# Products of token halves in three groups of the last block: seven for eight, in an attention and SwiGLU kernel

## Chip, cores and metric

One core of one Trainium2 chip runs the whole kernel. The metric is the device time of one execution in microseconds; three runs of the kernel before were timed, and the median counts.

## What is computed

```python
def reference(q, k, v, g_q, g_k, w_gate, w_val, w_out):      # q, k, v: (8, 12, 448, 64)
    scores = rmsnorm(q, g_q) @ rmsnorm(k, g_k).T / 8          # per batch and head
    x = softmax(scores) @ v                                   # heads side by side: (3584, 768)
    g = x @ w_gate                                            # (768, 1536)
    return (g / (1 + exp(-g)) * (x @ w_val)) @ w_out          # (1536, 768)
```

All of it is in float32.

## The kernel before

The function `fast` holds the kernel. The tokens are worked on in NB = 4 blocks of two batches (2 x 448 tokens). Each block has a *gate and value* stretch, x times both input matrices, and a *down* stretch, times the output matrix; the attention of the next two batches lies between the down products, and its preparation (squares, roots, transposes; `attention`, L736) reaches back into the gate and value stretch. The last block has no attention behind it.

The matrix products are made with a bilinear scheme that takes 15 products for 18 blocks: the two batches' tokens and three parts of the contraction are combined into 15 left sides, kept in the tile `xs` (L625), and the weights into 15 right sides, which the first block makes once and keeps in DRAM (`up_sides` L637, `down_sides` L638). The 15 are called by number; UP_ORDER (L627) is their order. The intermediate width of 1536 is cut into NG = 4 groups. So a gate and value stretch has 4 groups x 15 steps x 2 (gate and value) = 120 products (`up_product`, L1453). A product is NC2 = 2 calls of a 128x128 weight against 448 columns (L1474) and is planned at PRODUCT = 1.504 us (L665).

Each product accumulates onto a chain of earlier ones in its PSUM bank, and is read out after each step: by ScalarE as a copy (L1409) or by VectorE as a sum or difference with an earlier result (L1411, L1413, L1415), as UP_READ (L1394) says. Gate products use the two banks `mm`, value products the two banks `at`; chains are numbered so that steps alternate between the banks. Six results per group come out. For each, ScalarE takes the SiLU of the gate (L1551) and VectorE multiplies it with the value (L1554) into `gt`. The down products (`down_product`, L1639, matmul L1663) read `gt` and sums of it in `hs` (`combine`, L1612).

Weights for five steps are loaded from DRAM by one call of `up_load` (L1569) into one of two places `ws` (`load_sides`, L1417, DMAs at L1428), on the queue of SP. The rooms `work` (queries and keys, L580), `es` (softmax weights, L644) and `spare` are cut into named rings by `take` (L586).

The order of all work is made by a planner (`Order`, L365): each operation is added with an engine, a planned duration, a due time, what it comes after and which places it takes or uses; `run` goes through the engines and writes each engine's instructions out in the order in which they would start. On the chip every engine runs its own list in that order, and waits only for data and places. Due times come from block_start (L671), block_end (L674) and pair_time (L677).

Of the kernel before, what the change touches and what calls it, by code (L numbers as in the profile page):

```python
# [493 lines left out]
def fast(  # L494
# [45 lines left out]
    P = 128  # L540
# [27 lines left out]
        rr=4, ws=2, **{x + str(i): 1 for x in "vw" for i in range(6)},  # L568
# [14 lines left out]
    OFTEN = dict(w1=0, w2=1, w3=2, w4=3, rows=4)  # L583
# [82 lines left out]
    UP, DOWN, BOTH = 30 * NG * PRODUCT, 90.7, 170.0  # L666
# [3 lines left out]

    def block_start(n):  # L671
        return FIRST + n * (UP + BOTH) + MORE * (n > 0)

    def block_end(n):  # L674
        return block_start(n) + UP + MORE * (n == 0)
# [722 lines left out]
    }  # L1398
    DOWN_READ = {
# [17 lines left out]
    def load_sides(key, sides, part, sums):  # L1417

        n = 2 * (NC2 if sums is UP_SUMS else NG)
        to = take(*key, [P, WS])[:, 0 : n * len(part) * P]  # L1420
# [18 lines left out]
    def block(n):  # L1439
        add = order.add  # L1440
        start = block_start(n)
        unit = (block_end(n) - start) / (30 * NG)
# [10 lines left out]
        def up_product(g, step, x, which, load, key):  # L1453
            nonlocal last
            when = start + (2 * (15 * g + step) + which) * unit

            b = ("BCDAE".index(CHAIN[x]) % 2 if CHAIN[x] != "E" else 0) ^ (g % 2) ^ (n > 0)
            fresh = x in FRESH
            opens = which and g == 0 and step < 2
            at = place_of(x, UP_ORDER[step - step % 5 :][:5], UP_SUMS)  # L1460
            bank = (which, b)

# [5 lines left out]
            def emit():  # L1468
                if opens:
                    take(*value_banks[b], [P, TB])  # L1470
                w = tiles[key][:, 0 : 2 * NC2 * 5 * P]
                w = w.rearrange("p (w c x f) -> p w c x f", w=2, c=NC2, f=P)
                for c in range(NC2):
                    nc.tensor.matmul(  # L1474
                        ps(), w[:, which, c, at], xs[:, SLOT[x], c],
                        start=fresh and c == 0, stop=c == NC2 - 1, skip_group_check=True,
                    )
# [8 lines left out]
                uses=[key] + ([value_banks[b]] if which and not opens else []), mode="full",  # L1486
# [66 lines left out]
            def weigh():  # L1553
# [6 lines left out]
                "ACT", 0.55, when - 0.5, gate, after=[acc["gate", result]], takes=[act],  # L1560
# [5 lines left out]
                rank=60.0 * (n == 0),  # L1566
            )

        def up_load(g, piece):  # L1569
            key = ("ws", (n, g, piece))  # L1570
            load = add(
                "SP", 1.2, start + (30 * g + 10 * piece) * unit - 24.0,
                lambda: load_sides(key, up_sides[g], UP_ORDER[5 * piece :][:5], UP_SUMS),
# [289 lines left out]
```

## Time and profile before

| | |
|---|---|
| three runs | 1453.04, 1456.36, 1457.0 us; median 1456.36 us |
| span of the profiled execution | 1452.0 us, 19362 instructions (the page gives no other time for it) |
| TensorE matmul records | 6736, busy 1426.0 us |
| busy in the span: VectorE, ScalarE, GpSimd | 879.8, 601.6, 405.7 us |
| moved by DMA | 193.29 MB |

All times of the trace are counted from the start of the span. A `nc.tensor.matmul` call in float32 shows as two weight loads (PEld) and two matmul records (PE). DVE is VectorE, ACT ScalarE, POOL GpSimd; SPq is the DMA queue that SP issues to. Blocks start their gate and value stretches at about 124, 474, 827 and 1174 us.

### The profile page before, as it was taken

The page shows a single profiled execution, that of the slowest core. Times are in us where ns is not written, and L with a number is a line of the kernel's source. Part 1 is how long each engine was busy: PE and PEld are TensorE (multiplying, and loading weights), DVE is VectorE, ACT ScalarE, POOL GpSimd, SP SyncE. Part 2 cuts the span into 40 slices and gives each one's busy share as a digit, 9 for nine tenths or more (in the row PEclk, how much of TensorE's full clock was granted, in tenths as well). Part 3 has the DMA queues.
Part 4 walks back from the last instruction along what each step waited for, and adds up shares of the span by engine and source line. Part 5 has one row for each costly group of instructions (what it writes and reads, how often), then busy time and mean ns, then how long its engine had stood idle before and what let it go on. Part 6 is the DMA issues. An engine that isn't in the chain of part 4 may idle for free.

```text
span 1452.0 us, 19362 instructions
## 1 busy us (share of the span) xinstructions
PE 1426.0 (98%) x6736; PEld 689.5 (47%) x6736; DVE 879.8 (61%) x1485; ACT 601.6 (41%) x1210; POOL 405.7 (28%) x476
## 2 busy tenths in 40 slices
PE   8999999999999999999999999999999999999997
PEld 4455454534444455544444455544444445555553
DVE  5889876878866434546877642455686644442533
ACT  6875444476653222356564122345555322212100
POOL 4756666625443000022443200011434300000000
PEclk9999999999999999999999999999999999999999
DMA  7778979854643533433644623443463452322235
GB/s 196 217 219 268 352 266 310 260 149 90 129 103 64 133 102 92 114 113 70 122 98 86 138 74 107 107 112 93 85 126 77 95 135 73 108 73 90 69 100 110
DMA packets 410416, 193.29 MB, mean 133 GB/s; under 512 B 280004, under 2 KB 390852, under 8 KB 410308
## 3 DMA queue, kind: packets, MB, share of 16 engines
q1 hardware_dynamic: 399040, 190.57, 49.1%
q10 hardware_dynamic: 11140, 1.38, 0.7%
q8 instruction: 55, 0.90, 0.3%
q14 instruction: 53, 0.43, 0.1%
q0 software_dynamic: 128, 0.00, 0.0%
HBM read 157.29 MB, written 34.60 MB: 132 GB/s over the span
## 4 chain that ended last, share of the span: by engine, by line
PE 90%; DMA 3%; DVE 2%; ACT 2%; SPq 1%; issue 1%; POOL 1%; ACTq 0%; DVEq 0%; POOLq 0%
PE at L1474 25%; PE mm L1474 25%; PE mm L1663 23%; PE at L1049 8%; PE st L970 7%; PE st L1080 1%; PE mm L1080 1%; DMA out_dram<-spare 1%; SPq L768 1%; DMA work<-in_k_dram 1%; ACT es L985 1%; DMA xs<-in_moe_w_gate_dram 0%; PE st L908 0%; DMA v<-in_v_dram 0%; ACT work L918 0%
## 5 line engine op out<-in xcount | busy, mean ns | idle before, releaser
L1474 PE MATMUL at<-xs,ws 128*128 128x448 f32 x960 | 401.2, 540 | 2.5 <-DVE v L1413 1.4
L1474 PE MATMUL mm<-xs,ws 128*128 128x448 f32 x960 | 401.7, 541 | 0.2 <-DVE hs L1315 0.2
L1474 PEld LDWEIGHTS at<-xs,ws 128*128 128x128 f32 x960 | 181.4, 190 | 184.7 <-issue 166.7
L1474 PEld LDWEIGHTS mm<-xs,ws 128*128 128x128 f32 x960 | 182.2, 190 | 180.7 <-issue 177.9
L888 POOL TENSOR_TENSOR work<-work,rr 128x448 f32<-128x448 f32 x72 | 71.8, 1016 | 467.5 <-DVE rr L715 341.6
L1663 PE MATMUL mm<-gt,ws 128*128 128x448 f32 x448 | 175.5, 543 | 0.0
L970 PE MATMUL st<-work 64*64 64x448 f32 (+1 forms) x1536 | 151.2, 501 | 10.3 <-ACT work L918 4.9
L985 ACT ACTIVATE es<-st 128x896 f32<-128x896 f32 x129 | 114.2, 914 | 101.6 <-PE at L1049 87.8
L1411 DVE TENSOR_TENSOR gt<-gt,mm 128x448 f32<-128x448 f32 x64 | 39.7, 621 | 188.1 <-PE mm L1474 161.7
L1663 PE MATMUL mm<-hs,ws 128*128 128x448 f32 x384 | 151.3, 544 | 0.0
L990 POOL TENSOR_TENSOR sums<-es 128x896 f32<-128x896 f32 x36 | 77.2, 2145 | 176.8 <-PE st L1080 83.7
L1663 PEld LDWEIGHTS mm<-gt,ws 128*128 128x128 f32 x448 | 83.6, 190 | 83.0 <-issue 80.8
L1551 ACT ACTIVATE st<-gt 128x448 f32<-128x448 f32 x96 | 52.3, 547 | 159.1 <-DVE gt L1415 85.7
L1409 ACT COPY gt<-mm 128x448 f32<-128x448 f32 x80 | 42.6, 532 | 157.5 <-PE mm L1474 157.4
L1049 PE MATMUL at<-es,v 64*64 64x448 f32 (+1 forms) x1032 | 106.0, 507 | 0.0
L1663 PEld LDWEIGHTS mm<-hs,ws 128*128 128x128 f32 x384 | 71.3, 190 | 71.0 <-issue 70.1
L970 PEld LDWEIGHTS st<-work 64*64 64x64 f32 x1536 | 50.9, 133 | 79.1 <-issue 37.4
L1409 ACT COPY v<-at 128x448 f32<-128x448 f32 x96 | 51.0, 532 | 80.4 <-PE at L1474 79.6
L990 POOL TENSOR_TENSOR sums<-sums,es 128x896 f32<-128x896 f32 x36 | 76.0, 2112 | 2.8
L1049 PEld LDWEIGHTS at<-es,v 64*64 64x64 f32 (+1 forms) x1032 | 44.1, 134 | 56.2 <-issue 50.4
L1554 DVE SCALAR_TENSOR_TENSOR gt<-st,v 128x448 f32<-128x448 f32 x96 | 59.7, 622 | 7.3 <-DVE v L1415 0.5
L1411 DVE TENSOR_TENSOR v<-v,at 128x448 f32<-128x448 f32 x64 | 39.8, 621 | 39.6 <-PE at L1474 39.5
(170 smaller groups left out, 1550.5 us busy)
## 6 DMA issues: line engine op xcount, KB each, us to landing
ws<-up_sides SPq DMA_DIRECT2D x32, 1024.0 KB, 5.6
ws<-down_sides SPq DMA_DIRECT2D x16, 1024.0 KB, 5.7
ws<-down_sides SPq DMA_DIRECT2D x28, 512.0 KB, 4.8
ws<-up_sides SPq DMA_DIRECT2D x16, 768.0 KB, 4.9
out_dram<-spare SPq DMA_DIRECT2D x168, 56.0 KB, 2.1
v<-in_v_dram SPq DMA_DIRECT2D x96, 96.0 KB, 2.5
ws<-up_sides SPq DMA_DIRECT2D x32, 256.0 KB, 5.9
ws<-up_sides SPq DMA_DIRECT2D x16, 512.0 KB, 5.8
```

The source lines that it names most:

```text
L888: nc.gpsimd.tensor_tensor(out=tiles["t", m][:, x], in0=tiles["qk", (m, x)], in1=rr.to_broadcast([P, NC, C]), op=ALU.mult,)
L970: nc.tensor.matmul(st[ds(D * x, D), h, 0:n], tiles["KT", m][rows, ds(P * j + D * of_keys, D)], tiles["QT", m][rows, ds(Q * of_queries, n)] ...
L985: nc.scalar.activation(e, tiles["st", (m, j)][:, :, 0 : S * width(j) // P], AF.Exp)
L990: nc.gpsimd.tensor_tensor(out=to, in0=tiles["e", (m, 0)] if j == 1 else to, in1=e, op=ALU.add)
L1049: nc.tensor.matmul(tiles["at", (m, x)][ds(D * h, D), ds(0, Q) if early else queries], tiles["v", m][rows, j, h], tiles["e", (m, j)][rows, ...
L1080: nc.tensor.matmul(to[ds(D * h + C * x, C)], halves[:, x] if half else many[:, 0:C], term[:, h, 0:Q] if half else term[:, h, ts(x, Q)], st ...
L1409: nc.scalar.copy(to, ps)
L1411: nc.vector.tensor_tensor(out=to, in0=old, in1=ps, op=ALU.add)
L1474: nc.tensor.matmul(ps(), w[:, which, c, at], xs[:, SLOT[x], c], start=fresh and c == 0, stop=c == NC2 - 1, skip_group_check=True,)
L1551: nc.scalar.activation(take(*act, [P, 2, TB])[:, 0, 0:S], to, AF.Silu)
L1554: nc.vector.scalar_tensor_tensor(to, tiles[act][:, 0, 0:S], 1.0 / SCALE, tiles[ready], op0=ALU.mult, op1=ALU.mult,)
L1663: nc.tensor.matmul(banks[s][:, 0:S], w[:, s, g, at], where[x][:, g], start=fresh and g == 0, stop=g == NG - 1, skip_group_check=True,)
```

## The change

In the last block the order of the four groups' products changes, and groups 1 to 3 are computed in another way.

Group 0 is split: first its 15 gate products, at the end of the stretch its 15 value products. Between them come groups 1 to 3. For these, the tokens are cut into halves of 224 columns, and the two halves, the two parts of the contraction and the pair of gate and value make a 2 x 2 x 2 product, which is done in seven half products instead of eight. They run in four streams of each step: X (two half products: A11 and S2), Y (two: S1 and S3), Z (two: A12 and A22) and W (one: S4). Z and W follow two steps behind X and Y (LAG). Each stream has two PSUM banks.

GpSimd makes the sums S1 to S4 of token halves (`halves_of`), 60 operations of 224 columns, beside the gate products of group 0. S3 takes the place of half of `xs`, so `restore` puts that half back, 15 operations, before the value products. GpSimd also joins the streams' results for each of the six results of a group (`plus`, three to four operations of 224 columns and one of 448, the last of these on VectorE for three results of group 3), VectorE adds W's half (`top`), and the gate and the multiplication follow in place. Results of a group and the next have separate places for three to four of the six sums.

The seven right sides for each step are prepared in blocks 1 and 2 (`prepare`): 15 pieces of three steps, eight in block 1 and seven in block 2, 16 us apart. Each is loaded into `es` or the room of `t` and `QT` in turn, gets four subtractions of 384 columns on GpSimd and is stored in new DRAM tiles `up7`. In the last block they are loaded in pieces of three steps: four sides for X and Y (768 KB, three places) and three sides for Z and W (576 KB, two places), with `ws` and the room of `qk` as places.

The order of the table UP_SUMS changes so that three neighbouring steps lie together, and the place `ws` is one 128-column side wider. The sums of `gt` for the down products of all groups are made after the seven-product groups, since S1 lies in `hs`, and the down products take the groups in the order 1, 2, 3, 0. The core of the diff:

```diff
-        rr=4, ws=2, **{x + str(i): 1 for x in "vw" for i in range(6)},
+        rr=4, ws=2, **{x + str(i): 1 for x in "vw" for i in range(6)}, w6=1, **{x: 1 for x in ("xy0", "xy1", "xy2", "zw0", "zw1", "wl")},
...
-    OFTEN = dict(w1=0, w2=1, w3=2, w4=3, rows=4)
+    OFTEN = dict(w1=0, w2=1, w3=2, w4=3, rows=4, w6=7)
...
-    UP_SUMS = (8, 1, 7, 13, 10, 14, 3, 5, 11, 0, 4)
+    UP_SUMS = (8, 7, 1, 13, 10, 14, 3, 11, 4, 0, 5)
...
-    WS = 10 * NC2 * P
+    WS = 21 * P
...
+    SEVEN = {3: (1, 2, 3)}
+    HALF, LAG = S // 2, 2
+    up7 = {
+        g: dram.tile([P, 5, 7, 3, P], F32, name=f"up7_{g}")
+        for g in sorted({g for gs in SEVEN.values() for g in gs})
+    }
...
-    UP, DOWN, BOTH = 30 * NG * PRODUCT, 90.7, 170.0
+    DOWN, BOTH = 90.7, 170.0
...
+    SHORT = 40.0
+
+    def up_time(n, g=NG):
+        return sum(SHORT if i in SEVEN.get(n, ()) else 30 * PRODUCT for i in range(g))
...
+    PREPARE, PREPARE_PACE, up7_done = {1: [(g, u) for g in (1, 2, 3) for u in range(5)][:8], 2: [(g, u) for g in (1, 2, 3) for u in range(5)][8:]}, 16.0, {}
...
+        flat_hs = hs.rearrange("p s g t -> p (s g t)")
+        flat_es = es.rearrange("p n h t -> p (n h t)")
+        places_of = dict(S1=flat_hs, S2=work[:, 2 * NJ * 2 * D * 2 :], S4=flat_es)
+        held = [
...
+        def part_of(name, x):
+            tokens = slice(HALF, S) if name in ("A21", "A22", "S3") else slice(0, HALF)
+            if name[0] == "A" or name == "S3":
+                return xs[:, SLOT[x], int(name in ("A12", "A22")), tokens]
+            return places_of[name][:, ts(UP_ORDER.index(x), HALF)]
+
+        def halves_of():
+            for step, x in enumerate(UP_ORDER):
+                before = [old_done[x], *side_done[n, x], down_done.get(n - 1), clusters[EARLY * (n + 1) - 1, "total"]]
+                for i, (to, one, two, op) in enumerate((
+                    ("S3", "A11", "A21", ALU.subtract), ("S2", "A22", "S3", ALU.subtract),
+                    ("S1", "S2", "A11", ALU.add), ("S4", "A12", "S2", ALU.subtract),
+                )):
+                    done = order.add(
+                        "POOL", 0.66, start + (step + 1) * unit + 0.6 * i,
+                        lambda to=to, one=one, two=two, op=op, x=x: nc.gpsimd.tensor_tensor(
+                            out=part_of(to, x), in0=part_of(one, x), in1=part_of(two, x), op=op
+                        ),
+                        after=before, port=True, takes=held if step + i == 0 else [],
+                        uses=held if step + i else [],
+                    )
+                    before = [done]
+                    half_done[x, to] = done
+
+        def restore(now):
+            for step, x in enumerate(UP_ORDER):
+                side_done.setdefault((n, x), []).append(
+                    order.add(
+                        "POOL", 0.66, now - 3.0 + step * unit,
+                        lambda x=x: nc.gpsimd.tensor_tensor(
+                            out=part_of("A21", x), in0=part_of("A11", x), in1=part_of("S3", x),
+                            op=ALU.subtract,
+                        ),
+                        after=[third_done[x]], port=True, rank=30.0,
...
+        PARTS = dict(
+            X=((0, "A11"), (3, "S2")), Y=((2, "S1"), (1, "S3")),
+            Z=((0, "A12"), (2, "A22")), W=((1, "S4"),),
+        )
+        RESULT = {"t0": 0, "t1": 1, "d": 2, "t3": 3, "t4": 4, "t5": 5}
+
+        def sevens(begin_seven):
+            nonlocal last
+            q = PRODUCT / 4
+            steps, now = [], begin_seven
+            for k in range(15 * len(seven) + LAG):
+                for stream in "XYZW":
+                    j = k - LAG * (stream in "ZW")
+                    if 0 <= j < 15 * len(seven):
+                        steps.append((now, stream, j // 15, j % 15))
+                        now += q * len(PARTS[stream])
+
+
...
+            for (k, late), times in sorted(pieces.items(), key=lambda of: of[1][0]):
+                if late:
+                    at = (k - count) % 2
+                    name = f"zw{at}"
+                    base, tile_of = 12 * P, [ws_keys[at]]
+                else:
+                    at = (k - count + 2) % 3
+                    name = f"xy{at}"
+                    base, tile_of = (0, [ws_keys[at]]) if at < 2 else (4 * P, qk_keys)
+                key = name, (n, "seven", k)
...
+                    tiles[key] = room[:, base : base + (9 if late else 12) * P]
+                    src = up7[seven[k // 5]][:, k % 5, 4:7] if late else up7[seven[k // 5]][:, k % 5, 0:4]
...
+                g, x = seven[j], UP_ORDER[i]
+                b = ("BCDAE".index(CHAIN[x]) % 2 if CHAIN[x] != "E" else 0) ^ opening[stream == "Y"] ^ (j % 2)
+                bank = ({"X": 0, "Y": 1}.get(stream, stream), b)
+                fresh = x in FRESH
...
+                def emit(x=x, stream=stream, key=key, at=at, fresh=fresh, ps=ps, opens=opens, bank_tile=bank_tile):
+                    if opens:
+                        take(*bank_tile, [P, TB] if stream == "Y" else [P, 2, TB])
+                    w = tiles[key].rearrange("p (w x f) -> p w x f", x=3, f=P)
+                    for side, (slot, of) in enumerate(PARTS[stream]):
+                        nc.tensor.matmul(
+                            half(ps(), side), w[:, slot, at], part_of(of, x),
+                            start=fresh and side == 0, stop=True, skip_group_check=True,
...
+                    "PE", q * n_sides, when, emit,
+                    after=[
+                        load, last, free.get(bank),
+                        *(half_done[x, of] for _, of in PARTS[stream] if of[0] == "S"),
+                    ],
+                    takes=[bank_tile] if opens else [],
+                    uses=[key, *tile_of, *held] + ([bank_tile] if bank_tile and not opens else []), mode="full",
...
+                    if t == "t5" and other:
+                        return "sums", (n, g, t)
+                    if t == "t0" and other:
+                        return "v", (n, g, stream, t)
+                    if t == "t4" and other and (stream == "Y" or ends):
+                        return held[-1] if stream == "Y" else qk_keys[-1]
+                    if t == "t1" and other and stream == "Y":
+                        return "eh", (n, g, stream, t)
+                    X = {"t0": "v0", "t5": "v1", "t1": "v2", "t4": "v3", "t3": "v4", "d": "v5"}
+                    Y = {"t0": "w1", "t5": "w2", "t1": "w3", "t4": "w4", "t3": "rows", "d": "rows"}
...
+                    return order.add(engine, us, when, emit, after=after, uses=uses, port=True)
+
+                Xl, Xr, Yl, Yr, Wl = ("X", 0), ("X", 1), ("Y", 0), ("Y", 1), ("W", None)
+                closing = "DVE" if j == len(seven) - 1 and result in (2, 4, 5) else "POOL"
+                if stream == "X":
+                    ready7["X"] = plus(Xr, Xr, Xl, when + 1.0, [done], [kx])
+                elif stream == "Y":
+                    u4 = plus(Yl, Xr, Yl, when + 1.0, [done, ready7["X"]], [kx, ky])
+                    u3 = plus(Xr, Xr, Yr, when + 1.7, [u4], [kx, ky])
+                    ready7[g, result] = u3, plus(Yr, Yl, Yr, when + 2.4, [u3], [ky])
...
+                    def top(tile_at=tile_at, t=t):
+                        to = half(tile_at("Y", t), 0)
+                        of = flat_es[:, 15 * HALF :] if t == "t5" else tile_at("W", t)
+                        nc.vector.tensor_tensor(out=to, in0=to, in1=of, op=ALU.add)
+
+                    done = order.add(
+                        "DVE", 0.35, when + 3.0, top, after=[done, ready7[g, result][1]], uses=[ky, *(extra or [kw])], port=True, early=0.0, rank=20.0,
...
+                def load(four=four, part=part, g=g):
...
+                            for b in range(2):
+                                nc.sync.dma_start(
+                                    four[:, b, 0:2, ds(i * P, size * P)],
+                                    src[:, :, b].rearrange("p a x f -> p a (x f)"),
+                                )
+                            i += size
+
+                done = order.add(
+                    "SP", 1.0, when, load,
...
+                    moves=[transfer(2 * P, 4 * P * i) for i in groups(part, UP_SUMS) for _ in range(2)], early=0.0, **mine,
+                )
+                for i, (to, one, two) in enumerate(((2, 1, 0), (3, 5, 2), (1, 5, 1), (6, 4, 3))):
+                    done = order.add(
+                        "POOL", 0.92, when + 8.0 + i,
+                        lambda raw=raw, to=to, one=one, two=two: nc.gpsimd.tensor_tensor(
+                            out=raw[:, to], in0=raw[:, one], in1=raw[:, two], op=ALU.subtract
+                        ),
+                        after=[done], port=True, uses=keys[which],
+                    )
...
+                    "SP", 0.6, when + 14.0,
+                    lambda raw=raw, g=g, u=u: nc.sync.dma_start(
...
+        passes = [(g, (0, 1)) for g in range(NG) if g not in seven]
+        if seven:
+            passes[:1] = [(0, (0,)), None, (0, (1,))]
```

## Rows read from the trace of the kernel before

**Rows 1.** The page: busy time by engine, and the chain that ended last.

```profile
PE 1426.0 (98%) x6736; PEld 689.5 (47%) x6736; DVE 879.8 (61%) x1485; ACT 601.6 (41%) x1210; POOL 405.7 (28%) x476
...
PE 90%; DMA 3%; DVE 2%; ACT 2%; SPq 1%; issue 1%; POOL 1%; ACTq 0%; DVEq 0%; POOLq 0%
```

**Rows 2.** Stretches: us, busy us (x count) of PE, PEld, DVE, ACT, POOL; clock, DMA.

```profile
475.00:655.00 180.00, 180.00 (x515) 89.75 (x514) 78.01 (x138) 60.53 (x119) 11.94 (x10) 1.00 0.40 107
...
1177.00:1357.00 180.00, 180.00 (x480) 90.99 (x480) 69.85 (x113) 39.44 (x72) 0.00 (x0) 1.00 0.29 88
```

**Rows 3.** Timeline where the last block opens: start us, us, engine, line, operation.

```profile
1173.82 1.67 PE L1474 MATMUL mm<-xs,ws 128*128 128x448 f32 x4
...
1174.02 1.20 SPq L1428 DMA_DIRECT2D ws<-up_sides  x2
...
1175.24 0.63 DVE L1185 SCALAR_TENSOR_TENSOR xs<-xs 128x448 f32<-128x448 f32 x1
1175.33 1.67 PE L1474 MATMUL at<-xs,ws 128*128 128x448 f32 x4
...
1175.53 0.53 ACT L1409 COPY gt<-mm 128x448 f32<-128x448 f32 x1 [5.51 <-PE mm L1474]
```

**Rows 4.** Groups by shape, last block's gate and value stretch: count | busy us, mean ns.

```profile
L1474 PE MATMUL mm<-xs,ws 128*128 128x448 f32 x236 | 98.3, 539 | 0.0
...
L1474 PEld LDWEIGHTS mm<-xs,ws 128*128 128x128 f32 x235 | 44.6, 190 | 43.7 <-issue 43.7
L1554 DVE SCALAR_TENSOR_TENSOR gt<-st,v 128x448 f32<-128x448 f32 x24 | 15.0, 623 | 2.0
```

**Rows 5.** Timeline of the first stretch, narrow windows: short matmuls and weight loads.

```profile
8.42 0.19 PEld L1756 LDWEIGHTS mm<-rr,ident 112*128 112x128 f32 x1 [0.19 <-issue]
8.53 0.19 PEld L1756 LDWEIGHTS mm<-work,ident 112*128 112x128 f32 x1
...
10.27 0.37 PE L1756 MATMUL mm<-work,ident 112*128 112x224 f32 x1
...
10.27 0.56 PE L1756 MATMUL mm<-work,ident 112*128 112x224 f32 x2
...
10.28 0.19 PEld L1756 LDWEIGHTS mm<-work,ident 112*128 112x128 f32 x1
...
63.30 0.55 PE L1049 MATMUL at<-es,v 128*64 128x224 f32 x4
...
63.30 0.74 PE L1049 MATMUL at<-es,v 128*64 128x224 f32 x6
```

**Rows 6.** VectorE: two operations queued in the last block (timeline), and a short shape.

```profile
1208.60 0.62 DVE L1415 TENSOR_TENSOR gt<-mm,gt 128x448 f32<-128x448 f32 x1 [0.15 <-PE mm L1474]
1209.14 0.61 DVE L1554 SCALAR_TENSOR_TENSOR gt<-st,v 128x448 f32<-128x448 f32 x1
...
L714 DVE SCALAR_TENSOR_TENSOR ss<-ss,rr 128x28 f32<-128x28 f32 x36 | 6.8, 188 | 1.2
```

**Rows 7.** Lines by duration, ns min/median/max: GpSimd, and VectorE at 120 to 305.

```profile
L888 POOL TENSOR_TENSOR work<-work,rr x72: 936/941/2726, 291.1 to 1126.9; 128x448 f32<-128x448 f32 x72
...
L1336 POOL TENSOR_TENSOR es<-es x24: 447/456/735, 157.0 to 281.7; 128x128 f32<-128x128 f32 x20, 128x256 f32<-128x256 f32 x4
...
L1528 DVE TENSOR_TENSOR v<-v,v x3: 752/878/899, 166.3 to 251.0; 128x448 f32<-128x448 f32 x3
```

**Rows 8.** Waits inside 1170 to 1362: us in total, times, longest us.

```profile
PEld at L1474 <- DVE v L1411: 1.5, 8, 0.2
```

**Rows 9.** DMA issues: count, KB each, us to landing; loads of 1177 to 1357, stores.

```profile
ws<-up_sides SPq DMA_DIRECT2D x3, 768.0 KB, 4.8
...
up_sides<-hs SPq DMA_DIRECT2D x4, 960.0 KB, 5.4
```

**Rows 10.** ScalarE's timeline before the attention that follows block 1's products.

```profile
582.44 1.05 ACT L807 ACTIVATE work<-work 128x448 f32<-128x448 f32 x2
...
614.72 0.56 ACT L807 ACTIVATE work<-work 128x448 f32<-128x448 f32 x1
```

More of the change, by code (lines that the diff above doesn't have):

```diff
@@ L1417, in load_sides @@
     def load_sides(key, sides, part, sums):
-        n = 2 * (NC2 if sums is UP_SUMS else NG)
-        to = take(*key, [P, WS])[:, 0 : n * len(part) * P]
+        n = sides.shape[1] * (NC2 if sums is UP_SUMS else NG)
+        if key[0] == "qk":
+            tiles[key] = work[:, 4 * P :]
+        else:
+            take(*key, [P, WS])
+        to = tiles[key][:, 0 : n * len(part) * P]
         to = to.rearrange("p (n x f) -> p n x f", n=n, f=P)
@@ L1451, in block, with up_product @@
         acc = {}
-        def up_product(g, step, x, which, load, key):
+        def up_product(g, step, x, which, load, key, when, flip, alone):
             nonlocal last
-            when = start + (2 * (15 * g + step) + which) * unit
-            b = ("BCDAE".index(CHAIN[x]) % 2 if CHAIN[x] != "E" else 0) ^ (g % 2) ^ (n > 0)
+            b = ("BCDAE".index(CHAIN[x]) % 2 if CHAIN[x] != "E" else 0) ^ flip
             fresh = x in FRESH
-            opens = which and g == 0 and step < 2
             at = place_of(x, UP_ORDER[step - step % 5 :][:5], UP_SUMS)
             bank = (which, b)
+            opens = which and value_banks[b] not in opened
+            opened.update(value_banks[b : b + 1] * which)
             def ps():
@@ L1485, in up_product @@
                 takes=[value_banks[b]] if opens else [],
-                uses=[key] + ([value_banks[b]] if which and not opens else []), mode="full",
+                uses=[*users[key]] + ([value_banks[b]] if which and not opens else []), mode="full",
             )
@@ L1559, in up_product @@
             gated = add(
-                "ACT", 0.55, when - 0.5, gate, after=[acc["gate", result]], takes=[act],
+                "ACT", 0.55, when - 0.5, gate, after=[acc["gate", result], seven_done[0]], takes=[act],
                 mode="silu", rank=60.0 * (n == 0),
@@ L1576, in up_load @@
                 early=8.0, rank=SIDES_RANK,
             )
+            users[key] = [key, *more]
             last_load[:] = [load]
             return key, load
-        for g in range(NG):
-            steps = [(step, which) for step in range(15) for which in range(2)]
+        turn_of = [int(n > 0)] * 2
+        opened = set()
+        old_done, half_done, hs_free = {}, {}, [None]
+        flat_hs = hs.rearrange("p s g t -> p (s g t)")
+        flat_es = es.rearrange("p n h t -> p (n h t)")
@@ new lines, in block @@
+        passes = [(g, (0, 1)) for g in range(NG) if g not in seven]
+        if seven:
+            passes[:1] = [(0, (0,)), None, (0, (1,))]
+        users, now = {}, start
+        for one in passes:
+            if one is None:
+                halves_of()
+                begin_seven = now
+                sevens(begin_seven)
+                seven_done[:] = [last]
+                now += SHORT * len(seven)
+                group_end.update({g: now - SHORT * (len(seven) - 1 - i) for i, g in enumerate(seven)})
+                restore(now)
+                continue
+            g, of_pass = one
+            steps = [(step, which) for step in range(15) for which in of_pass]
@@ L1589, in block @@
+            now += len(steps) * unit
+            group_end.pop(g, None)
+            group_end[g] = now
+        if n in PREPARE:
+            prepare()
         up_done[n] = last
@@ L1610, in block, with combine @@
         products = down_products
-        def combine(x, one, two, op, when, after, g=None):
+        def combine(x, one, two, op, when, after, g=None, rank=0.0):
             to = where[x]
```

250 lines of the change are left out of this document (226 added, 24 removed).

## Prediction

> **What bounds the kernel now.** I read the page's busy line and its chain first: TensorE is busy 98% of the span, and 90% of the chain that ended last is TensorE's own work [rows 1]. Then the busy time by stretch. In a middle gate and value stretch and in the last one TensorE is busy 180.0 of 180.0 us, VectorE 78 and 70, ScalarE 61 and 39, GpSimd 12 and 0 [rows 2]. So the last block's stretch is pure matmul streaming with an idle GpSimd beside it, and only fewer or shorter matmuls can shorten it. The timeline where that stretch opens gives the pace: one product (four matmul records, since each call appears as two) starts at 1173.82, the next at 1175.33, so 1.505 us a product [rows 3]. The groups by shape say the same: 448-column matmuls with a record of 539 ns, weight loads of 190 ns lying under them [rows 4]. 180.0 us over the 480 matmul records of that stretch is 0.375 us each.
>
> **TensorE's part of the change.** Removed: in groups 1 to 3, 3 x 30 products = 90 x 1.505 = 135.4 us. Added: per group and step seven calls of 224 columns, 3 x 15 x 7 = 315 calls = 630 matmul records. No 128x128 matmul of 224 columns stands in the trace in a stream, so I bound its interval. Below: two 224-column records one behind the other end the pair at 0.56 us where one alone takes 0.37, so they are 0.19 apart, with a weight load starting 0.01 after the first; in a stream the 224-column pairs on half the columns grow from 0.55 to 0.74 us as two more records come in, again 0.19 per pair [rows 5]. Above: a weight load that is not covered at all. Two loads of 128 columns start at 8.42 and 8.53, so a load holds its place for 0.11 us, and the interval would be 0.19 + 0.11 = 0.30 [rows 5]. I take 0.189, half of the full interval plus a rounding, since the row with the same width and 128 weight columns is the nearest one. 630 x 0.189 = 119.1 us. **Gain 135.4 - 119.1 = 16.3 us.** The upper end, 630 x 0.30 = 189 us, would be 54 us slower; the range leaves that end out, since the row of the same width shows otherwise, and rival 2 takes a part of it. The value products of group 0 move behind the seven-product groups at the same price, 15 x 1.505, and four sums feeding the down products change order at no TensorE cost.
>
> The Trainium skill (TensorE: Matmul & The Clock Gate, Back-to-back issue gap) says that in a stream of weight loads and matmuls both set the spacing, and gives about 81 ns a matmul at 128 columns where streaming alone is about 56. Taken over as 25 ns on each of the 630 records that would be an estimated 16 us, the whole gain. This trace speaks against it: 0.19 us apart with a load between [rows 5].
>
> **VectorE and ScalarE in the seven-product groups.** Per step four banks are read instead of two. Nine of fifteen steps read on VectorE: 448 columns cost 623 ns by record, and 0.54 us start to start when queued; 28 columns cost 188 ns, so 224 columns by a straight line 0.39 [rows 4, 6]. Per group 9 x (3 x 0.62 + 0.39) = 20.3, the extra additions 3 x 0.62 + 0.39 = 2.3, six short sums 2.3, six multiplications 3.7: 28.6 of 39.7 us. It fits, but it bunches: steps 10 to 14 are all VectorE reads, 5 x 2.25 + 2.3 = 13.5 us in 5 x 2.65 = 13.2. A stream's bank is wanted again two steps later, some 4.5 us after its product, which covers such a knot. ScalarE has six copies per stream and six gates, about 15 of 39.7 us.
>
> **GpSimd.** It takes all the new sums. A 448-column sum has a median of 941 ns, a 128-column one 456, so 224 columns 0.60 and 384 columns 0.84 us [rows 7]. The operand halves are 60 x 0.60 = 36 us; they start one product behind the gate pass (22.6 us) and are wanted at the pace 2.65 us per step against 2.4 us of work, so the last is done some 18 us early: no cost. Each result needs 4 x 0.60 + 0.94 = 3.3 us, five of them in steps 10 to 14, 16.7 against 13.2 us: the rest runs into the next group's first steps, where the second places for sums keep the copies from waiting for it. With both engines on SBUF operands the sums stretch: GpSimd's up to 2726 from 941 ns, VectorE's to a median of 878 in the first block [rows 7] against 623 [rows 4]. Sixteen operations a group work so, 16 x 0.26 = 4 us, which makes VectorE's share 32.7 of 39.7 us. I put the waits of TensorE in three groups at 1.5 us, between 0 (bank slack covers all) and 8.
>
> The Trainium skill (SBUF — State Buffer, Who interferes with whom) says that a VectorE instruction with two SBUF inputs and a GpSimd one that reads SBUF exclude each other for the whole instruction. The stretched records agree that they hinder each other; were each of the sixteen to wait a whole 0.94 us sum, VectorE would need 28.6 + 15 = 43.6 us a group and be the bound, as in rival 3.
>
> **The two passes of group 0.** Alone, a pass uses two banks, so a bank is wanted again 1.50 us after its product. The read starts 0.20 us after the next product's start, 1175.53 against 1175.33 [rows 3], and takes 0.62; 0.6 us is spare. The gate pass opens with four ScalarE copies and VectorE's last token sum starts at 1175.24 [rows 3], before that is wanted. In the value pass nine reads share VectorE with about twenty other operations; one ahead of a read is free, two cost some 0.5. TensorE's weight-load side shows such waits at 1.5 us in eight [rows 8]. I take 1.0, bounds 0 and 5.
>
> **DMAs and SP's queue.** SP moves past: gate weights alone (piece 1 issued at 1174.02, as now [rows 3], but wanted 7.5 instead of 15 us into the block), the seven-group pieces, value pieces, and the first down piece 7.5 instead of 15 us ahead. 768 KB land in 4.8 us [rows 9], so these hold by about 2 us. The tightest is the first piece behind the gate pass: its room frees at 22.6 us and it is wanted 5.7 us later. I take 0.5 us, bounds 0 and 2. Later pieces have 7.9 us or more.
>
> **Blocks 1 and 2.** Fifteen pieces are loaded, turned by 4 sums each (60 x 0.84 = 51 us on a GpSimd with 12 us of work per stretch) and stored. 960 KB stored take 5.4 us [rows 9], so 1344 KB about 7.5, where the planner counts some 4. VectorE and TensorE do not wait for any of it. What it holds is the room of the attention's operands: in block 1 until about 611. Its eighth store goes out 4 + 7 x 16 + 14 = 130 us after the block's start near 474. Now the squares of the first pair run at 582.44, and the next of its pieces goes at 614.72 [rows 10], so the cover is nearly used up; a ScalarE square 3 us late has the copies queued behind it and through them TensorE. I take 0.5 us for both blocks, bounds 0.5 gained by a changed order and 6 lost. Table order, widths and planner figures cost nothing: the loads stay contiguous and TensorE covers them.
>
> **Sum.** 16.3 - 1.5 - 1.0 - 0.5 - 0.5 = 12.8 us. The profiled execution spans 1452.0 us, 1.0 below the fastest and 4.4 below the median run of 1456.4; its new span would be 1439.2, and with the same 4.4 around it **1443.6 us**.
>
> **Rivals.** (1) *Covers break in part*: two passes with 4 us, blocks 1 and 2 with 3, groups 3: 16.3 - 10 - 0.5 leaves about 6, 1450. For it speak the 0.6 us of spare per bank; against it the few waits in rows 8. Chance 0.19. (2) *Weight loads show at 224 columns*: if a fifth of the 0.11 us showed, 630 x 0.022 = 13.9 us leave 2.4 of the gain, less than the 3.5 us of waits above: 1457, no change. Against it stands the 0.19 of rows 5. Chance 0.07. (The Trainium skill's rule on the issue gap, cited above, is this case.) (3) *Slower: VectorE waits in order for GpSimd.* The short top sum and the multiplication wait for three GpSimd sums, and bank reads queue behind them. At 941 ns GpSimd needs 16.7 us for five results. If contention makes it 1.5 times as long, 25 us, VectorE's head is some 12 us late, 4.5 are covered, 7.5 are lost per group: 22 us against 16.3, and with the other terms (2 us) 1464. It decides from about 1.4 times on. For it: the stretched records in rows 7; against it: the medians there, within 2% of the minima. Chance 0.07. (4) *Nothing waits at all*: 16.3 + 0.5, 1439.5, chance 0.05. The forecast keeps 0.62.
>
> **Numbers.** A measurement of this kernel tells 0.3%, about 4.4 us, from no change. Faster: forecast, (4) and most of (1), 0.84. Within it: the worst of (1) and most of (2), 0.07. Slower: (3) and the rest of (2), 0.09. The range runs from 1438.5 (nothing waits) to 1452.5 (case 1 with its upper bounds); what is left out is (2) and (3) and the edge of (1).
>
> **What would show it.** Right: the last block's gate and value stretch about 164 us instead of 180.5, its 224-column matmul starts 0.19 apart; GpSimd about 105 us busy in it (36 + 60 + 9 for putting the tokens back); the down products unchanged. Wrong: starts 0.2 or more apart with a weight load before each; TensorE idle behind VectorE's short sums, or VectorE idle behind GpSimd; ScalarE's squares idle behind the stores in blocks 1 and 2, with copies and TensorE behind them; the first piece of the seven-product groups landing after the gate pass.

## The result, and the profile after

The changed kernel takes 1459.21 us (median of 8 runs, 1457.0 to 1462.23), the kernel before 1455.88 us (8 runs beside it): ratio 1.0027, interval 1.0017 to 1.0038, so 3.3 us more, where 12.8 less had been forecast. The profiled executions span 1457.7 and 1452.0 us.

The page of the kernel after, busy time by engine (against [rows 1]):

```profile
span 1457.7 us, 20499 instructions
...
PE 1415.0 (97%) x7006; PEld 738.0 (51%) x7006; DVE 927.1 (64%) x1566; ACT 612.3 (42%) x1244; POOL 581.2 (40%) x698
```

TensorE is busy for 11 us less, as a saving of products must give, and the program is longer all the same: idle time has come in. The windows of the last block's stretch say how much (columns as in [rows 2]):

```profile
1174.00:1355.00 181.00, 170.29 (x756) 141.04 (x755) 113.32 (x193) 51.19 (x106) 117.15 (x162) 1.00 0.43 142
```

TensorE was busy 180.0 of 180.0 us here before. Now 10.7 us are idle, at a granted clock of 1.00, and no other engine is full. (Busy time understates the saving a little: a product that stands alone counts 1.74 us, as below, one in a row of products 1.505.) The stretch has three parts, whose borders are the first products in the timeline: the gate pass of group 0 takes 1177.73 to 1200.28, 22.55 us for 15 products of 1.505, without a gap; the seven-product groups 1200.28 to 1322.00, 121.7 us; the value pass 1322.00 to 1358.26, 36.3 us, where 22.6 would do. Together 180.5 us, against 180.4 before.

The groups first, where the pace was the forecast's main term. The timeline of the kernel after, TensorE in the first step:

```profile
1200.28 0.54 PE L1750 MATMUL mm<-xs,work 128*128 128x224 f32 x2
1200.28 0.19 PEld L1750 LDWEIGHTS mm<-xs,work 128*128 128x128 f32 x1 [0.19 <-issue]
...
1200.66 0.54 PE L1750 MATMUL mm<-work 128*128 128x224 f32 x2
...
1201.04 0.54 PE L1750 MATMUL at<-hs,work 128*128 128x224 f32 x2
...
1201.41 0.54 PE L1750 MATMUL at<-xs,work 128*128 128x224 f32 x2
```

Two records take 0.375 to 0.38 us from start to start, so 0.189 each, with the weight loads under them. 630 x 0.189 = 119.1, and 2.65 us of the 121.7 are waits.

Then the value pass. The timeline of TensorE there, kernel after (in brackets the idle time before, and what ended it):

```profile
1322.00 1.67 PE L1496 MATMUL at<-xs,work 128*128 128x448 f32 x4
1324.33 1.74 PE L1496 MATMUL at<-xs,work 128*128 128x448 f32 x4 [0.67 <-issue]
1326.79 1.74 PE L1496 MATMUL at<-xs,work 128*128 128x448 f32 x4 [0.71 <-ACT v L1424]
1329.24 1.74 PE L1496 MATMUL at<-xs,work 128*128 128x448 f32 x4 [0.71 <-ACT v L1424]
1331.70 1.74 PE L1496 MATMUL at<-xs,work 128*128 128x448 f32 x4 [0.71 <-ACT v L1424]
```

From the second on, each of these starts some 2.45 us after the one before it: 1.74 us of product, then 0.71 us in which its result is read. The one released is the product directly behind. With two banks it should have been the second one behind. A few lines further the timeline shows both sides of such a step:

```profile
1341.50 1.74 PE L1496 MATMUL at<-xs,ws 128*128 128x448 f32 x4 [0.88 <-DVE v L1426]
1343.28 0.62 DVE L1426 TENSOR_TENSOR v<-v,at 128x448 f32<-128x448 f32 x1 [1.39 <-PE at L1496]
...
1344.05 1.74 PE L1496 MATMUL at<-xs,ws 128*128 128x448 f32 x4 [0.81 <-DVE v L1426]
```

TensorE waits for VectorE and VectorE for TensorE in turn: product, read, product, read. At one place of the pass two products do run in a row; presumably the first one's read was planned behind the second product:

```profile
1334.27 3.25 PE L1496 MATMUL at<-xs,ws 128*128 128x448 f32 x8 [0.83 <-POOLq L2240]
1337.55 0.62 DVE L1426 TENSOR_TENSOR v<-v,at 128x448 f32<-128x448 f32 x1 [2.85 <-PE at L1496]
...
1338.20 0.53 ACT L1424 COPY v<-at 128x448 f32<-128x448 f32 x1 [6.17 <-DVE v L1426]
...
1338.88 1.74 PE L1496 MATMUL at<-xs,ws 128*128 128x448 f32 x4 [1.37 <-ACT v L1424]
```

The read of the first of the two is VectorE's. It starts at 1337.55, when the second product has ended, and not some 1.5 us earlier, when its own had; VectorE was idle for 2.85 us. So the read waited for the product in the other bank too, and little is gained. The chain that ended last, in order of time (start, us, what), has the same alternation up to the first down product:

```profile
1353.36 0.76 issue
1354.13 1.76 PE at L1496 x4
1355.88 0.02 issue
1355.90 0.64 DVE v L1430
1356.54 0.14 issue
1356.68 1.74 PE at L1496 x4
1358.42 75.18 PE mm L2072 x200
```

The code offers a reason. The two `mm` banks are two tiles, the two `at` banks are the halves of one tile (L659 after, `at_banks = psum.tile([P, 2, TB], ...)`). If the wait is kept for the tile, a product into one half waits for the read of the other, and a read of one half for the product into the other. Each half has 512 columns (TB), as much as an `mm` tile.

Last, the other parts of the program. Each length is the difference of two first products in the timelines, in us; "rest" runs from the first down product of the last block to the span's end.

| kernel | block 0 | block 1: gate and value | block 1 | block 2 | last stretch | rest |
|---|---|---|---|---|---|---|
| before | 356.0 | 185.3 | 347.3 | 346.9 | 180.4 | 97.8 |
| after | 358.4 | 188.5 | 348.4 | 347.4 | 180.5 | 99.4 |
| value products on `mm` | 356.8 | 188.5 | 348.2 | 347.3 | 168.2 | 99.5 |
| preparation alone | 359.4 | 188.5 | 348.6 | 347.4 | 180.4 | 97.8 |
| preparation again | 357.5 | 188.5 | 348.3 | 347.7 | 180.4 | 97.8 |
| tables alone | 359.4 | 185.3 | 346.6 | 346.4 | 180.4 | 97.8 |
| preparation planned only | 358.9 | 188.5 | 347.6 | 347.4 | 180.4 | 97.8 |
| value products on `mm`, pieces 12 us apart | 358.7 | 188.0 | 350.4 | 346.5 | 167.7 | 98.9 |
| preparation alone, pieces 12 us apart | 357.3 | 187.1 | 349.0 | 346.8 | 180.4 | 97.8 |

Block 0 has the same order of instructions in all of them and scatters by 3.4 us, so a difference of that size in one profile says nothing. Among kernels with the same order of work in them, blocks 1 and 2 scatter by 1 us at most, the last two columns hardly at all.

### The profile page after: what moved, and what is told of

The parts are those of the page before. It is cut to its first block, busy times and chain, and to the rows that moved or that the text cites. A ratio compares the mean times of both kernels' runs of the same rounds, so it can differ in the third digit from the quotient of the medians.

```text
span 1457.7 us, 20499 instructions
## 1 busy us (share of the span) xinstructions
PE 1415.0 (97%) x7006; PEld 738.0 (51%) x7006; DVE 927.1 (64%) x1566; ACT 612.3 (42%) x1244; POOL 581.2 (40%) x698
## 5 line engine op out<-in xcount | busy, mean ns | idle before, releaser
L1496 PE MATMUL at<-xs,ws 128*128 128x448 f32 x760 | 318.5, 542 | 12.5 <-DVE v L1428 4.5
L1496 PE MATMUL mm<-xs,ws 128*128 128x448 f32 x780 | 324.5, 542 | 0.2 <-DVE hs L1329 0.2
L1496 PEld LDWEIGHTS at<-xs,ws 128*128 128x128 f32 x760 | 142.6, 190 | 160.6 <-issue 140.8
L1496 PEld LDWEIGHTS mm<-xs,ws 128*128 128x128 f32 x780 | 148.4, 191 | 146.7 <-issue 143.8
L1426 DVE TENSOR_TENSOR gt<-gt,mm 128x448 f32<-128x448 f32 x52 | 32.3, 621 | 134.4 <-PE mm L1496 132.6
L1573 ACT ACTIVATE st<-gt 128x448 f32<-128x448 f32 x78 | 42.5, 547 | 131.4 <-DVE gt L1430 62.9
L1424 ACT COPY gt<-mm 128x448 f32<-128x448 f32 x65 | 34.6, 532 | 123.1 <-PE mm L1496 122.9
L1953 POOL TENSOR_TENSOR es<-es 128x384 f32<-128x384 f32 x32 | 31.3, 1001 | 118.3 <-DMA es<-up_sides 93.0
L1424 ACT COPY v<-at 128x448 f32<-128x448 f32 x80 | 42.5, 532 | 75.8 <-PE at L1496 68.1
L936 DVE STREAM_TRANSPOSE work<-work 128x448 f32<-128x448 f32 x72 | 45.6, 638 | 24.9 <-POOL work L902 20.7
```

The costliest lines, as they stand in the source:

```text
L936: nc.vector.transpose(to, tiles["t", m][:, x].rearrange("p c f -> p (c f)"))
L1424: nc.scalar.copy(to, ps)
L1426: nc.vector.tensor_tensor(out=to, in0=old, in1=ps, op=ALU.add)
L1496: nc.tensor.matmul(ps(), w[:, 0 if alone else which, c, at], xs[:, SLOT[x], c], start=fresh and c == 0, stop=c == NC2 - 1, skip_group_chec ...
L1573: nc.scalar.activation(take(*act, [P, 2, TB])[:, 0, 0:S], to, AF.Silu)
L1953: lambda raw=raw, to=to, one=one, two=two: nc.gpsimd.tensor_tensor(out=raw[:, to], in0=raw[:, one], in1=raw[:, two], op=ALU.subtract),
```

## Experiments

**Value products on the other banks.** Theory A: the halves of one tile make the products wait. The edit gives the lone passes the banks `mm` (cut to its core):

```diff
+            pair = 0 if alone else which
-            bank = (which, b)
+            bank = (pair, b)
...
-                if which == 0:
+                if pair == 0:
                     return banks[b][:, 0:S]
...
-            flips = list(turn_of)
-            for which in of_pass:
+            flips = [turn_of[0]] * 2 if len(of_pass) == 1 else list(turn_of)
+            for which in (0,) if len(of_pass) == 1 else of_pass:
```

> The value products of group 0 write to the two banks mm, which are two tiles, instead of the two banks at, which are halves of one tile. Theory A (a product into one half of a shared tile waits for the last read of the other half, so the pass runs product, read, product): the value pass falls from 36.3 us to between 22.6 and 24, its products start 1.50 us apart, and the time falls by 12 to 14 us, to about 1446. Rival B (the pass waits because VectorE and ScalarE are crowded with the last group's sums there): the products stay 2.4 to 2.6 us apart, and the time stays near 1459.

Measured: 1445.6 us (1444.26 to 1449.08), ratio to before 0.9944 (0.993 to 0.9958). That is 13.6 us under the changed kernel's median, or some 12 us if both are taken by their ratios to the kernel before, which ran beside each. The value pass takes 1320.36 to 1344.31, 24.0 us. Windows of the pass, this kernel, and then the kernel after:

```profile
1320.40:1344.30 23.90, 22.91 (x61) 11.09 (x59) 20.28 (x33) 7.77 (x15) 8.92 (x11) 1.00 0.25 72
```

```profile
1322.00:1358.20 36.20, 25.59 (x61) 10.33 (x60) 19.52 (x31) 7.78 (x15) 9.12 (x11) 1.00 0.17 48
```

VectorE and ScalarE have the same work in both (20.28 and 19.52, 7.77 and 7.78 us). In 24 us it fits beside TensorE; so the crowd on VectorE is not what held the pass. Five products in a row stand in one line of this timeline, 20 records in 7.68 us. Two waits make up the 1.4 us over 22.6: about half a microsecond for a GpSimd sum, and 0.9 us of the first down product, which needs the bank of the last value product:

```profile
1320.36 7.68 PE L1497 MATMUL mm<-xs,work 128*128 128x448 f32 x20
...
1329.83 13.77 PE L1497 MATMUL mm<-xs,ws 128*128 128x448 f32 x36 [0.28 <-POOL sums L1862]
1344.31 1.02 PE L2073 MATMUL mm<-hs,ws 128*128 128x448 f32 x2 [0.71 <-DVE v L1428]
```

**Gate products on the `at` banks.** The opposite edit (`pair = 1 if alone else which`): a pass with nearly idle readers is put on the suspected banks, and the value pass stays there.

> The changed kernel with the gate products of group 0 on the two banks at (halves of one tile) instead of the two banks mm; the value pass as in the changed kernel. VectorE and ScalarE have little to do in the gate pass. Theory A (shared tile): the gate pass stretches from 22.55 us to between 34 and 38, products about 2.5 us apart, and the time grows by 12 to 15 us, to about 1473. Rival B (crowded engines): the gate pass stays at 22.6 us and the time near 1459.

Measured: 1471.44 us (1470.58 to 1472.4), ratio 1.0117 (1.0101 to 1.0132), 12.2 us more than the changed kernel (13 by the ratios to before); the gate pass takes 13.4 us longer. Its gate pass, windows and timeline:

```profile
1176.94:1212.88 35.94, 26.29 (x61) 10.25 (x60) 9.49 (x15) 3.19 (x6) 33.85 (x53) 1.00 0.31 88
```

```profile
1179.23 1.77 PE L1497 MATMUL at<-xs,ws 128*128 128x448 f32 x4 [0.62 <-ACT gt L1424]
...
1181.03 0.53 ACT L1424 COPY gt<-at 128x448 f32<-128x448 f32 x1 [1.86 <-PE at L1497]
...
1181.62 1.77 PE L1497 MATMUL at<-xs,ws 128*128 128x448 f32 x4 [0.62 <-ACT gt L1424]
```

VectorE is busy 9.5 and ScalarE 3.2 of 35.9 us, the products are still 2.39 us apart, and the copy starts when its product is done. Nothing is late; the order itself is serial.

**The `mm` banks as one tile.** Is it the tile, or these two banks? Starting from the kernel with value products on `mm`:

```diff
-    banks = [psum.tile([P, TB], F32, name=f"mm{i}", bufs=1) for i in range(2)]
+    both = psum.tile([P, 2, TB], F32, name="mm", bufs=1); banks = [both[:, i] for i in range(2)]
```

> The kernel with the value products of group 0 on the banks mm, in which these two banks are now halves of one tile, as the banks at are; both passes of group 0 and the down products run on them alone. Theory A in its narrower form (a product into one half of a tile waits for the last read of the other half, whichever banks these are): products 2.4 to 2.6 us apart in both passes, so 36 us instead of 22.6 for the gate pass and 36 instead of 24.0 for the value pass, and the down products slower as well. Rival (it is these particular banks, at, that are slow to be written beside a read): both passes stay at 22.6 and 24 us.

Measured: 1561.92 us in its one run, beside 1456.12 for the kernel before. The gate pass takes 1236.85 to 1273.77, 36.9 us, and the value pass 1395.99 to 1433.12, 37.1 us; the timeline of TensorE in the gate pass has the pattern seen above, now on the fast banks:

```profile
1241.63 1.77 PE L1497 MATMUL mm<-xs,ws 128*128 128x448 f32 x4 [0.62 <-ACT gt L1424]
1244.02 1.77 PE L1497 MATMUL mm<-xs,ws 128*128 128x448 f32 x4 [0.62 <-ACT gt L1424]
1246.41 1.77 PE L1497 MATMUL mm<-xs,ws 128*128 128x448 f32 x4 [0.62 <-ACT gt L1424]
1248.97 1.77 PE L1497 MATMUL mm<-xs,ws 128*128 128x448 f32 x4 [0.78 <-DVE gt L1426]
```

With one tile the fast banks are slow. The wait belongs to the tile, and the rival falls.

**The preparation alone.** With `SEVEN = {}` the last block is as before, while blocks 1 and 2 still make and store the seven right sides.

> The last block as before the change, with the fifteen pieces of right sides still loaded, summed and stored in blocks 1 and 2 (nobody reads them). What the preparation costs by itself: the profile of the changed kernel shows blocks 1 and 2 longer by 1.0 and 0.5 us, so 1457 to 1458 against 1456 for the kernel before. If the 3.9 us by which the last block opened late in the changed kernel were the preparation's own price, it would be about 1460.

Measured: 1458.27 us beside 1454.12 for the kernel before, ratio 1.0024 (1.0014 to 1.0035): 3.5 us over it, nearer to the 3.9 of the second answer than to the first. Run again on another chip:

> The preparation alone once more, on the same chip as the three parts: 3 to 4 us over the kernel before, as in its first run (ratio 1.0024).

Measured: 1456.74 us beside 1455.32, ratio 1.0013 (1.0002 to 1.0024): 1.9 us, below the 3 to 4 expected. So 1.9 to 3.5 us, where the forecast had 0.5; the two intervals together reach from 0.3 to 5 us.

**Tables alone.** The same without the call of `prepare()`: only the new table order, the widths and the planner's figures are left.

> Only the new order of the table of right sides, the wider weight place and the new rooms; no preparation, the last block as before the change. Each engine's list of instructions is that of the kernel before, but for the strides of eight pairs of GpSimd sums per converted piece. In the profiles so far block 0, whose list does not change, took 356.8 to 359.4 us with the new table against 356.0 before. Theory C (the table's strides shift GpSimd and VectorE in block 0 so that they meet): about 2 us slower than before, 1456.5 to 1457.5 beside 1454 to 1455, block 0 about 358. Rival D (the loss in block 0 is chance, the preparation costs its 1.5 us in blocks 1 and 2 and the rest is noise): no difference, within 1 us of the kernel before.

Measured: 1455.16 us against 1454.73, ratio 1.0 (0.9992 to 1.0009). The tables cost nothing that can be told (1.3 us at most); the preparation does.

**Pieces 12 instead of 16 us apart**, `PREPARE_PACE` 12.0: in the kernel with the value products on `mm` (there also with the last value product on the other bank), and in the preparation alone.

> The value products on the two banks mm, the last of them on the bank that the first down product does not use, and the fifteen pieces 12 us apart instead of 16, so that block 1's rooms are free some 28 us earlier. If the 1.5 us in blocks 1 and 2 come from rooms that the attention's preparation gets late: 1.5 us off, and 0.7 us off by the last bank, so 1443 to 1444 against 1445.6 for the value products on mm alone, 0.7% faster than the kernel before. If they come from the work of the pieces itself (GpSimd beside VectorE, SP's queue): only 0.7 us off, about 1445.

> The preparation alone with the pieces 12 us apart, the last block as before the change. Late rooms: blocks 1 and 2 as long as before (347.3 and 346.9 us), the time 1.5 us below the preparation alone at 16 us (1458.3), so about 1456.5 to 1457. Work of the pieces themselves: blocks 1 and 2 still 1.0 and 0.5 us longer, 1458.

Measured: 1446.37 us, ratio 0.9935 (0.9922 to 0.9948), and 1458.13 us, ratio 1.002 (1.0009 to 1.003). Both are level with their kernels at 16 us, while late rooms would have made them 1.5 us faster. Nor are their blocks as long as before: block 1 takes 350.4 and 349.0 us (347.3 before), block 2 346.5 and 346.8. The room that the pieces hold until late, on which the forecast had built its 0.5 us, is not the cost. Of the gain from the last bank the trace has 0.5 us in the last stretch (167.7 for 168.2); block 1, 2.2 us longer than at 16 us, takes it back.

**The preparation in parts.** The planner adds the same pieces with the same costs, but some of them issue nothing; TensorE's list stays that of the preparation alone:

```diff
-                def load(four=four, part=part, g=g):
-                    i = 0
+                def load(four=four, part=part, g=g, j=j):
+                    i = 0 if j < 0 else 9
...
-                        if here:
+                        if here and i < 9:
...
-                        lambda raw=raw, to=to, one=one, two=two: nc.gpsimd.tensor_tensor(
+                        lambda raw=raw, to=to, one=one, two=two: None and nc.gpsimd.tensor_tensor(
...
-                    lambda raw=raw, g=g, u=u: nc.sync.dma_start(
+                    lambda raw=raw, g=g, u=u: None and nc.sync.dma_start(
```

> The preparation is planned in blocks 1 and 2 with all its costs and places, but none of its loads, sums and stores is issued; the right sides it would make are wanted by nothing in this kernel, whose last block is as before. TensorE's list is that of the preparation alone, instruction for instruction. Theory E (the other order costs the time: TensorE meets ScalarE's exponentials 0.2 to 1.0 us late): as the preparation alone, 3 to 4 us over the kernel before, and the first block's gate and value stretch of 188.5 us stays. Rival F (the transfers or the sums themselves cost it): within 0.5 us of the kernel before.

> As the preparation alone, with its loads and stores but without its 60 GpSimd sums (the stored right sides are not the right ones, and nothing reads them). Theory E: 3 to 4 us over the kernel before, as with nothing issued. Rival F by transfers: 3 to 4 us as well, but only if the planned-only kernel is level; rival F by sums (GpSimd and VectorE hinder each other): within 0.5 us of the kernel before.

> As the preparation alone, with its 60 GpSimd sums but without its stores and with only the first load of each place and block (the right sides are not made). Theory E: 3 to 4 us over the kernel before. Rival F by transfers: within 0.5 us of the kernel before; rival F by sums: 3 to 4 us, but only if the planned-only kernel is level.

Measured, ratios to before: planned only 1.0013 (1.0004 to 1.0022), without sums 1.0017 (1.0008 to 1.0026), nearly without transfers 1.0007 (0.9996 to 1.0018), whole 1.0013 (1.0002 to 1.0024). Sums and transfers that are not there take nothing away that can be told. The lone plan costs about 1.9 us, less than the 3 to 4 expected, and these intervals overlap, so the order is shown to cost something, not that it is all. The other order can be seen in block 1 (which the expectation calls the first block): groups of TensorE's work in its gate and value stretch, kernel before, then planned only.

```profile
L970 PE MATMUL st<-work 64*64 64x448 f32 (+1 forms) x48 | 4.5, 486 | 0.0
```

```profile
L984 PE MATMUL st<-work 64*64 64x448 f32 (+1 forms) x64 | 6.6, 505 | 0.5 <-ACT es L999 0.5
L1063 PE MATMUL at<-es,v 64*64 64x448 f32 x8 | 1.0, 552 | 0.0
```

The planner, with GpSimd and SP booked, starts the next attention's score products earlier against the gate products. The stretch grows by 3.1 us (188.5 for 185.3 in the table, in every kernel with 16 us of pace), and the down stretch, which has that work no longer, gives back some 2. TensorE's waits for ScalarE's exponentials in blocks 1 and 2 sum to 2.3 us before, 2.7 planned only and 3.2 after; the rest of the 1.9 to 3.5 us was not located.

## Why the prediction was wrong

**The step that failed** is in "The two passes of group 0": "Alone, a pass uses two banks, so a bank is wanted again 1.50 us after its product [...] 0.6 us is spare", and from it "I take 1.0, bounds 0 and 5". The passes cost 13.7 us, all in the value pass (36.26 - 15 x 1.505), of which the banks' shared tile makes 12.3, since on two tiles it is 24.0 us. The count of two banks came from the schedule, but what the wait is kept for came from nowhere: the gate pass, on two tiles, kept the 1.50 us that the step claims for both. That `at` is one tile stood in the code (L650 of the kernel before). In the kernel before, a gate product stands between any two value products, so a value product comes 3.01 us behind the last and the wait of about 0.9 us is covered.

It had left a mark in [rows 8], but not the one that the prediction read. The timeline of the kernel before at one of these places:

```profile
1195.07 0.53 ACT L1409 COPY v<-at 128x448 f32<-128x448 f32 x1 [0.97 <-PE at L1474]
...
1196.00 0.19 PEld L1474 LDWEIGHTS at<-xs,ws 128*128 128x128 f32 x1 [0.19 <-issue]
...
1198.15 0.62 DVE L1411 TENSOR_TENSOR v<-v,at 128x448 f32<-128x448 f32 x1 [0.88 <-PE at L1474]
...
1199.01 0.19 PEld L1474 LDWEIGHTS at<-xs,ws 128*128 128x128 f32 x1 [0.19 <-DVE v L1411]
...
1199.38 1.67 PE L1474 MATMUL at<-xs,ws 128*128 128x448 f32 x4
```

The 0.19 us are no lost time: the same gap stands in front of a weight load that nobody holds up (1196.00), and the pace stays 1.505 us. So the 1.5 us in eight that the prediction took as the size of such waits measure nothing. What the row does tell is a name. The product of 1199.38 writes the half that ScalarE had emptied by 1195.60; the read named, VectorE's at 1198.15, is that of the other half. The trace has it throughout: each of the 58 value products of this stretch that follow two others waits for a signal of the engine that read the other half, also the 23 whose own half another engine had read. There was a wait for it with a cover, and the change takes away the cover.

The other terms, in order:

- **TensorE's gain of 16.3 us: right.** 0.189 us a record was taken from [rows 5] and 0.189 was measured; the gate pass adds nothing. Rival 2 (weight loads show) falls: a record with its 0.19 us load keeps the pace of the columns.
- **Waits in the three groups, 1.5 us (0 to 8): 2.65.** Within bounds. In the main the same cause: the streams Y, Z and W too have their two banks in one tile, so what is waited for is wanted again one step later, where the prediction counted two steps ("some 4.5 us") for every stream. Most steps cover that. In the last steps of the last group, where nothing else comes between, TensorE stops twice for the read of the step before, about 0.6 us each from start to start:

```profile
1320.76 1.02 PE L1750 MATMUL st<-xs,ws 128*128 128x224 f32 x4 [0.34 <-DVE gt L1430]
```

(timeline of TensorE, kernel after, 1.2 us before the groups end.) Two of Y's products (1236.62 and 1276.74) lose 0.3 to 0.4 us each in the same way.

- **GpSimd**: 117 us busy in the stretch against "about 105". A 224-column sum takes 0.66 us where a line through [rows 7] gave 0.60. Of TensorE's waits only two, some 0.2 us each in the first steps of the groups, are put down to a GpSimd sum. Rival 3 (VectorE queues behind GpSimd by 22 us) falls: the waits for VectorE just named come to about 2 us in all.
- **DMAs and SP's queue, 0.5 us: none.** The first piece behind the gate pass is there in time; TensorE goes on at 1200.28 without a gap, and no later gap of the groups is put down to a DMA.
- **Blocks 1 and 2, 0.5 us (-0.5 to 6): 1.9 to 3.5.** Within bounds, for another reason than the one given: not the room held late (the 12 us pace changes nothing), but at least partly the planner's other order. The prediction named that order only as a possible gain.
- **Not in the sum: 1.6 us at the end.** From the first down product to the end of the span it is 99.4 and 99.5 us in the kernels with the seven products (98.9 in the one with its pieces 12 us apart) and 97.8 in those without. The last transposition ends 91.7 us after that product in the kernel before and the one after, so the time lies behind all computation. The instructions in the trace place it: among those with which SP closes the program, two neighbours stand 1.65 us apart (1454.54 to 1456.18), where it is 0.05 us in the kernel before; in the kernel with 98.9 the widest such gap is 0.85. Why SP stops there, no run here separates.

The range's lower end, 1438.5, is called "nothing waits", which rival 4 puts at 1439.5; nothing hangs on it.

The sum with the measured terms: 16.3 - 2.65 - 13.7 - (1.9 to 3.5) - 1.6 = 3.6 to 5.2 us slower, against 3.3 measured (2.5 to 5.5 by the interval). Case 1 (covers break in part) had the right place and allowed 4 us for the passes; no case had a pass that loses its whole overlap.

With the value products on `mm` the same sum reads 16.3 - 2.65 - 1.4 - (1.9 to 3.5) - 1.6 = 7.2 to 8.8 us faster, and 0.56% or 8.1 us were measured. That kernel beats both.

## What to carry to other kernels

When a reorder puts next to each other what was interleaved, look in the old trace for who releases whom, even where no time is lost: gaps of 0.2 us that every weight load has named the read of the other half, and with it a wait of 0.9 us whose cover the reorder removed. Compare such a gap with its neighbours before its length is taken for a wait. Count places of a ring by what the waits are kept for, the tile here, and not by the banks in the hardware; two accumulators that should overlap need two tiles. And price planned work by the order it makes as well as by the work, since an order made from costs changes where these are booked.

## What the runs showed that was not expected

The granularity of the wait itself: one line of the program, two banks as one tile, is worth 12.3 us in one pass, and 116 us (1561.92, one run, against 1445.6) when it is done to the `mm` banks, which both passes, all down products and the opening use.

VectorE's operations with both inputs in SBUF can stretch by more than the 0.26 us that the prediction added each, when GpSimd sums run beside them. Groups of the kernel after in the seven-product groups, by shape:

```profile
L1903 DVE SCALAR_TENSOR_TENSOR gt<-gt,spare 128x448 f32<-128x448 f32 x8 | 6.9, 887 | 0.3
L1891 DVE TENSOR_TENSOR spare<-spare 128x224 f32<-128x224 f32 x5 | 5.3, 1059 | 0.0
```

The same 224-column sum took 384 ns where it met no GpSimd operation, the multiplication 618. It cost TensorE little (Y's two waits above stand behind stretched sums), because VectorE had the time to spare.
